# Half of the first batch's k and q before the rest, halved light attention, and new planner constants in a fused attention and feed-forward kernel

## The chip, the cores and the metric

The kernel runs on one core of a Trainium2 chip. The metric is the device time of one execution in microseconds (us); three timed runs are given by their median. A core has five engines that run side by side, each its own list of instructions in order: TensorE (PE in the profile, with its weight loads as PEld), VectorE (DVE), ScalarE (ACT), GpSimd (POOL) and SyncE (SP), which here issues the loads, the stores and the DMA transposes. They wait for one another by semaphores. PE writes to PSUM, which has eight banks in this kernel, all of them named; the other data lie in SBUF.

## The reference

Sliding window attention feeds a feed-forward block with a squared ReLU. There are 8 batches of 576 tokens, 8 heads of 64.

```python
scores = scale * np.matmul(q, k.transpose(0, 1, 3, 2))          # scale 1/8
mask = np.abs(pos[:, None] - pos[None, :]) <= 32
scores = np.where(mask, scores, -1000000000.0)
scores = scores - np.max(scores, axis=-1, keepdims=True)
attn = np.exp(scores)
attn = attn / (np.sum(attn, axis=-1, keepdims=True) + 1e-09)
x = np.matmul(attn, v)                  # then to (4608 tokens, 512)
h = x @ w_in                            # 512 x 2048
r = np.maximum(h, 0.0)
g = s * (r * r) + b
return (g @ w_out).astype(np.float32)   # 2048 x 512
```

All inputs and the output are float32. The kernel computes the matrix products in bfloat16. It uses that s and b are scalars: out = s * (r*r @ w_out) + b * (column sums of w_out).

## The kernel before

**Tiles.** The 4,608 tokens form 36 attention tiles of 128 (index j). The feed-forward part takes six tiles of 128 tokens and then fifteen of 256. The first product (`ht`, line 1015) is done in groups of 16 matmuls of 128 columns or 8 of 256; ACT takes the ReLU of a group (line 1024), DVE squares it into GT (line 1043). The second product (line 1063) is done in four groups of four matmuls per 128 tokens, one for each quarter of w_out; DVE scales it and adds the constant (line 1077), SP stores it. The column sums of w_out (line 940) need all of w_out.

**Weights.** w_in and w_out are loaded as float32 in four chunks of 1 MB each (i0 to i3, o0 to o3), into parts of GT or of the output buffers that are not in use yet, and are cast to bfloat16 by four casts a chunk. `WSET` (line 291) names the engines that may cast: ACT and POOL. The next chunk in the same place waits for the casts of the one before.

**The first batch.** k and q of batch 0 come as raw float32 (`load_raw`, line 568): partition h*16 + c holds 36 consecutive tokens of head h. Each of k and q is loaded in two halves, a half holding 18 tokens out of each 36. They are cast by eight pieces of 288 columns (`turn_raw`, line 577), turned by matmuls against a permutation matrix PERM in five groups, and copied into TURN (`kwt`, `qwt`), where the tokens lie along the free dimension. Every tile of the first batch that reads TURN waits for all of it (`turns`, line 673).

**Attention.** Tiles 0 to 2 use `attend_light` (line 681): scores with the mask added by a matmul, one maximum per row (DVE, line 704), the same scores transposed, from which the maxima are taken off by a small matmul (line 740), exp on ACT straight into the transposed form (line 746), row sums by matmuls, then the product with v, one division (line 775), a turn back (line 782) and a copy to XT. Even and odd heads lie in two PSUM banks, but each step takes both. The other tiles use `attend` (line 793): DVE adds the mask and takes the maximum for each head (line 832), ACT takes exp and the sum (line 840), POOL or, in the first five tiles, also DVE multiplies by the reciprocal (line 854), and P is transposed by PE for tiles below `PDMA` and by a DMA transpose on SP's queue from there on (line 868). k and q of later batches are cast by POOL (`cast_kq`), v by POOL or DVE (`cast_v`, line 636); for tiles below 12 a second copy VO of v with the halves exchanged is made by ACT or DVE (`make_vo`, line 641).

**What sets the order.** All work is entered as nodes with a cost in ns, a key, and what it reads and writes. `_Plan.order` (line 103) lays the nodes out engine by engine: whenever an engine is free by its own clock, it takes the ready node with the smallest key; a node with several engines (`move`, line 547) goes to the one that would finish it first. The result is a fixed list for each engine; on the chip each engine goes through it in order. `akey(j)` (line 305) is the key of attention tile j, min(640, 600 + 60j) tokens ahead of the same tokens' first product. `room` (line 112) models how many DMA descriptors SP may have outstanding, `RING`, `ISSUE` and `LAND` (line 25) how long a load takes. `FIRST` (line 289) is the order of the first loads: K0 is the first half of k, v0 the first tile of v; what stands behind the n-th bar is entered with tile n-1's attention. Where PE would idle early, filler matmuls (line 462) are put in.

## Time and profile before

| what | value |
|---|---|
| timed runs | 317.75 us median of 3 (317.01 to 319.76) |
| profiled execution | 316.46 us |
| its span, first to last instruction | 314.7 us |
| granted TensorE clock | 1.00 throughout |
| PE, DVE, ACT, POOL busy | 300.8, 229.0, 230.0, 145.5 us |
| moved by DMA | 61.82 MB |

The profiled execution's own time is 316.46 us: 1.8 us lie around its span. Busy times are sums over the span; matmuls overlap one another, so a busy PE may still be doing little. In the rows by stage, the columns are the stage, its length, and the busy time of each engine with the number of instructions in brackets, then the granted clock, the share of the 16 DMA engines' time (which can pass 1) and GB/s. In the rows in order of time, the first number is the start, the second how long the piece lasts; brackets at the end give how long the engine was idle before it and what it waited for. "x16" counts instructions merged into a row.

### The profile page before, as it was taken

The numbers are of one execution on the slowest core, as the hardware profiler recorded it, in microseconds if no ns is written. First come the engines' busy times: TensorE is split into PE (matmuls) and PEld (weight loads), VectorE is DVE, ScalarE is ACT, GpSimd is POOL, SyncE is SP. The second block draws the span as 40 slices with busy tenths as digits, with TensorE's granted clock in tenths as the row PEclk, the third lists the DMA queues.
The fourth block names the chain that finished last, engine by engine and source line by source line (L and its number), as shares of the span: only waits on it lengthen the run. The fifth ranks groups of instructions, "written<-read, shape, count | busy, mean of one in ns | idle before, by whom it ended". The sixth has DMA issues, their size and how long they took to land.

```text
span 314.7 us, 10141 instructions
## 1 busy us (share of the span) xinstructions
PE 300.8 (96%) x3936; PEld 207.4 (66%) x3981; DVE 229.0 (73%) x897; ACT 230.0 (73%) x747; POOL 145.5 (46%) x192
## 2 busy tenths in 40 slices
PE   7899899998999999999999999999999999999996
PEld 3468657586667665776666766666666666676674
DVE  5779499899998778677766787678858767653242
ACT  5577866899797868698787878798878778835230
POOL 7233476556575534445454654655654532220000
PEclk9999999999999999999999999999999999999999
DMA  7998999999999999999999999899999562220011
GB/s 273 359 351 228 361 268 214 240 229 179 210 213 210 232 187 197 223 227 176 191 218 226 210 205 233 217 192 226 225 247 204 123 149 70 70 67 35 33 69 68
DMA packets 157125, 61.82 MB, mean 196 GB/s; under 512 B 131220, under 2 KB 147988, under 8 KB 157076
## 3 DMA queue, kind: packets, MB, share of 16 engines
q1 hardware_dynamic: 157072, 61.16, 90.7%
q8 instruction: 31, 0.51, 0.7%
q14 instruction: 18, 0.15, 0.2%
q10 hardware_dynamic: 4, 0.00, 0.0%
HBM read 37.03 MB, written 9.44 MB: 148 GB/s over the span
## 4 chain that ended last, share of the span: by engine, by line
PE 77%; DMA 7%; DVE 7%; ACT 3%; POOL 2%; issue 2%; SPq 1%
PE ht L1015 35%; PE ptp L1063 15%; PE outp L1063 15%; DMA gt<-in_moe_w_out_dram 3%; PE sc L820 3%; DMA v<-in_v_dram 2%; ACT p L840 2%; PE sc L1063 2%; DMA r32k<-in_k_dram 2%; PE av L1063 2%; DVE ss L832 1%; PE tp L909 1%; PE av L915 1%; DVE mx L704 1%; DVE outs L1077 1%
## 5 line engine op out<-in xcount | busy, mean ns | idle before, releaser
L1015 PE MATMUL ht<-xt,win 128*128 128x256 bf16 (+1 forms) x1344 | 146.5, 257 | 0.0
L1015 PEld LDWEIGHTS ht<-xt,win 128*128 128x128 bf16 x1344 | 115.1, 98 | 32.7
L1024 ACT ACTIVATE r<-ht 128x512 bf16<-128x512 f32 x144 | 85.1, 592 | 47.3 <-PE ht L1015 45.8
L1043 DVE TENSOR_TENSOR gt<-r 128x512 bf16<-128x512 bf16 x144 | 83.6, 583 | 48.7 <-ACT r L1024 47.1
L840 ACT ACTIVATE p<-ss,mx 128x128 bf16<-128x128 f32 x264 | 110.0, 420 | 7.6 <-DVE mx L832 6.9
L854 POOL TENSOR_TENSOR p<-p,rc 128x512 bf16<-128x512 bf16 x64 | 70.0, 1114 | 77.5 <-DVE rc L849 77.5
L832 DVE CUSTOM_DVE_ANT_0 ss<-sc,mask 128x128 f32<-128x128 f32 x264 | 62.0, 280 | 8.8 <-PE sc L820 8.4
L1063 PE MATMUL outp<-wout,gt 128*128 128x512 bf16 (+1 forms) x246 | 63.0, 372 | 3.9 <-issue 1.7
L1063 PE MATMUL ptp<-wout,gt 128*128 128x512 bf16 x240 | 61.9, 379 | 1.7 <-issue 1.3
L840 ACT ACTIVATION_READ_ACCUMULATOR p<-ss,mx 128x1 f32 x264 | 50.2, 190 | 0.0
L1063 PEld LDWEIGHTS outp<-wout,gt 128*128 128x128 bf16 x272 | 24.9, 98 | 19.3 <-ACT wout L556 1.0
L1063 PEld LDWEIGHTS ptp<-wout,gt 128*128 128x128 bf16 x256 | 24.1, 98 | 19.3
L551 POOL CAST kn<-r32k 128x512 bf16<-128x512 f32 x34 | 21.1, 646 | 23.9 <-DMA r32k<-in_k_dram 23.9
L551 POOL CAST qn<-r32q 128x512 bf16<-128x512 f32 x32 | 21.3, 665 | 9.9 <-DMA r32q<-in_q_dram 9.5
L832 DVE DVE_READ_ACCUMULATOR2_ANT mx<- 128x1 f32 x264 | 20.8, 79 | 0.0
L924 ACT COPY half<-tp 128x512 f32<-128x512 f32 x24 | 14.0, 583 | 9.2 <-PE av L915 8.8
L551 POOL CAST ve<-v 128x512 bf16<-128x512 f32 x27 | 18.0, 667 | 3.3 <-PE av L915 2.5
L926 DVE TENSOR_TENSOR xt<-av,half 128x512 bf16<-128x512 f32 x24 | 16.3, 681 | 0.9 <-ACT half L924 0.8
L820 PEld LDWEIGHTS sc<-kt,qt 64*64 64x64 bf16 x768 | 10.8, 108 | 8.7 <-issue 7.8
L820 PE MATMUL sc<-kt,qt 64*64 64x64 bf16 (+1 forms) x768 | 14.2, 204 | 0.0
L846 DVE TENSOR_SCALAR sm<-sm 128x8 f32<-128x8 f32 x33 | 6.7, 202 | 8.9 <-ACT p L840 8.8
L1077 DVE SCALAR_TENSOR_TENSOR outs<-outp,scb,cvec 128x512 f32<-128x512 f32 (+1 forms) x17 | 12.4, 728 | 0.9 <-PE outp L1063 0.9
(142 smaller groups left out, 237.3 us busy)
## 6 DMA issues: line engine op xcount, KB each, us to landing
out_dram<-outs SPq DMA_DIRECT2D x35, 256.0 KB, 3.8
v<-in_v_dram SPq DMA_DIRECT2D x28, 256.0 KB, 5.5
r32q<-in_q_dram SPq DMA_DIRECT2D x28, 256.0 KB, 5.2
r32k<-in_k_dram SPq DMA_DIRECT2D x9, 512.0 KB, 4.7
gt<-in_moe_w_in_dram SPq DMA_DIRECT2D x4, 1024.0 KB, 10.6
gt<-in_moe_w_out_dram SPq DMA_DIRECT2D x3, 1024.0 KB, 9.7
v<-in_v_dram SPq DMA_DIRECT2D x8, 192.0 KB, 5.1
r32k<-in_k_dram SPq DMA_DIRECT2D x3, 448.0 KB, 4.8
```

Of the source, the lines that this page charges most:

```text
L551: return e.tensor_copy(dst, src)
L820: r = e.matmul(SC[hh][64 * u:64 * u + 64, pr, x0:x1], lhsT=qq, rhs=kk, start=True, stop=True)
L832: lambda e, ss=ss, x=x, y=y, pr=pr, hh=hh: e.tensor_tensor_reduce(out=SS[ss][:, x, :], in0=SC[hh][:, pr, :], in1=MASK[kind][:, :], scale=- ...
L840: lambda e, ss=ss, x=x, y=y: e.activation(P[pb][:, y, :].rearrange("q (a p t) -> q a p t", a=2, t=2), spread(SS[ss][:, x, :]), AF.Exp, bia ...
L854: return e.tensor_tensor(P[pb][:, y0:y0 + 4, :], P[pb][:, y0:y0 + 4, :], RC[mb][:, y0:y0 + 4].unsqueeze(2).broadcast_to([128, 4, 128]), AL ...
L924: add("act", lambda e: e.copy(HALF[hb][:, :], AV2[:, :]), 620, key + AVK, reads=[AV2N], writes=[("HALF", hb)])
L926: add("dve", lambda e: e.tensor_tensor(XT[:, :, 128 * (j % NX):128 * (j % NX) + 128], AV[:, :, :], HALF[hb][:, :].rearrange("p (a b) -> p ...
L1015: r = e.matmul(hbank[:, nt * f:nt * f + nt], lhsT=WIN[:, kc, 128 * ft:128 * ft + 128], rhs=XT[:, kc, x0:x0 + nt], start=(kc == 0), stop=(k ...
L1024: return e.activation(R1[rb][:, :], hbank[:, :], AF.Relu, bias=0.0, scale=1.0)
L1043: return e.tensor_tensor(d, r, r, ALU.mult)
L1063: r = e.matmul(op_[:, 0:cn], lhsT=GT[:, g_, fc, :], rhs=WOUT[:, fc, c0:c0 + cn], start=(fc == 0), stop=(fc == 15))
L1077: add("dve", lambda e, ob=ob, op_=op_, c0=c0, cn=cn: e.scalar_tensor_tensor(OUTS[ob][:, 0:cn], op_[:, 0:cn], SCB[:, 0:1], CVEC[:, c0:c0 + cn],
```

## The change

- **Loads of the first batch.** A half of k or q is now a half of the tokens: first 288 tokens, then the other 288. The 16 chunks of 18 tokens are the outer dimension, the heads the inner one, so a partition is c*8 + h and PERM is built for that. The order of the loads is Q0, K0, K1, v0, v1, Q1 instead of K0, K1, Q0, Q1, v0, v1. Each half is cast and turned by itself, in three groups of 6 tokens; tiles 0 and 1 wait only for the first halves, and the second halves get later keys. The bfloat16 copies lie where P and the scores lie later, not in XT.
- **Order of the loads after that.** v4 goes from before o0 to before o3; q4 and q5 come after k2 and before o1.
- **Light attention by halves.** Each step of `attend_light` is split into one for the even heads and one for the odd ones; the row sums move into the same bank as the product with v.
- **Who does what.** Weights may also be cast by DVE, the VO copies by POOL too; casts of v from tile 12 on are POOL's alone; POOL may take squares of the first four tiles; PE's transposes of P go up to tile 4 instead of 3 (`PDMA` 5); DVE's share of the normalisation goes up to tile 5.
- **The scalars s and b** are spread over the partitions after tile 1's attention instead of at the start.
- **Planner.** Costs of most operations are changed (ACT's ReLU 490 instead of 600, DVE's square 400 instead of 440, and so on), the latency behind an instruction is 230 instead of 130 (190 on POOL), a load lands after 1200 instead of 2000, a queue entry counts in full until it is done. There is a rule to leave an engine idle for a better node that is ready soon, switched off by `LOOK` = 0. The lead of attention is min(640, 500 + 40j).

What the built lists of the instructions show:

| engine | before | after |
|---|---|---|
| DVE: casts of weights | 0 | 16 |
| ACT: casts of weights | 16 | 7 |
| POOL: casts of weights | 16 | 9 |
| POOL: casts and copies of v | 27 | 40 |
| DVE: casts and copies of v | 25 | 14 |
| SP: DMA transposes of P | 32 | 31 |
| PE: filler matmuls | 16 | 10 |

```diff
-START, RING, ISSUE, LAND = 800.0, 2400.0, 700.0, 2000.0
+START, RING, ISSUE, LAND = 800.0, 2400.0, 700.0, 1200.0
-HOLD, DEFER, CHANGE = 800.0, 200.0, 97.0
+HOLD, DEFER, CHANGE = 100.0, 200.0, 97.0
+LOOK, LOOK_GAP, LOOK_END = 0.0, 50.0, 30000.0
...
-            while sum(q * min(1.0, (end - t) / dur) for end, dur, q in queue if end > t) + nd > RING:
+            while sum(q for end, dur, q in queue if end > t) + nd > RING:
...
-    LEAD, L0, LS = 640, 600, 60
-    RELU, SQ = 500, 200
-    FIRST = "K0 K1 Q0 Q1 v0 v1 i0 i1 i2 v2 i3 v3 v4|q4 o0 k2 o1 o2 q5 o3|v5|||"
+    LEAD, L0, LS = 640, 500, 40
+    NSQ = 4
+    RELU, SQ = 300, 400
+    FIRST = "Q0 K0 K1 v0 v1 Q1 i0 i1 i2 v2 i3 v3 o0 k2|q4 q5 o1 o2 v4 o3 v5||||"
-    WSET = {"i": ("pool", "act"), "o": ("act", "pool")}
-    NFLEX, TAIL = 8, 3
-    PDMA, KQDMA, AHEAD, GATE = 4, 11, 4, 5
-    CKEY, SKEY = 200, -9250
+    WSET = {"i": ("pool", "act", "dve"), "o": ("act", "pool", "dve")}
+    VOP = 12
+    HSTEP, CB, VOK = 0.1, -500, -100
+    NFLEX, TAIL = 10, 3
+    PDMA, KQDMA, AHEAD, GATE = 5, 11, 4, 5
+    CKEY, SKEY = 100, -9450
-    WHOLE, LIGHT, CH, NDIV = 4, 3, S // 16, 5
+    HC, HT_ = -600, 150
+    WHOLE, LIGHT, CH, NDIV = 4, 3, S // 16, 6
...
     def VSET(j):
-        return ("pool", "dve")
-    def OSET(j):
-        return ("act", "dve")
+        return ("pool",) if j >= 12 else ("pool", "dve")
+    def OSET(j, r0):
+        return ANY if r0 == 0 and j < VOP else ("act", "dve")
...
-            src = {"K": k, "Q": q}[x][0].rearrange("h (c r) d -> (h c) (r d)", r=CH)
+            src = {"K": k, "Q": q}[x][0][:, S // 2 * half:S // 2 * half + S // 2, :].rearrange(
+                "h (c r) d -> c h (r d)", c=16)
...
+        def turn_raw(x, half):
+            flat, out, late = FLAT[x], TURN[x], 0 if x == "K" else 50
+            step, n = CH * D // 8, CH // 6
+            ckey_, tkey = (-9500, -9400) if half == 0 else (HC, akey(2) - HT_)
...
-        turns = [("TURN", x, i) for x in "KQ" for i in range(5)] + ["KPAD"]
+        def turns(j):
+            return ["KPAD"] + [("TURN", x, half, i) for x in "KQ" for half in range(2 if j > 1 else 1)
+                               for i in range(3)]
...
+            for hh in range(2):
+                h_ = hh * HSTEP
+                pts = [("PTS", ptb, y) for y in range(hh, 8, 2)]
+                turned[j] = add("pe", partial(av, hh=hh), 500, key + 3 + h_,
...
+                add("dve", lambda e, hh=hh: e.reciprocal(RC[mb][:, hh:8:2], AVB[hh][:, 256:260]), 120,
...
-                    add("act", relu, 600, key - RELU, reads=[hres], writes=[("R1", rb)])
+                    add("act", relu, 490, key - RELU, reads=[hres], writes=[("R1", rb)])
...
-                add("dve", sq, 440, key - SQ, reads=[("R1", rb)],
+                few = t0 < 128 * NSQ
+                add(("dve", "pool") if few else "dve", {"dve": sq, "pool": sq} if few else sq,
+                    {"dve": 400.0, "pool": 1100.0} if few else 400, key - SQ, reads=[("R1", rb)],
```

## The prediction

> **What bounds the kernel now.** I read the page first (who is busy, and the chain that ended last), then the busy time by stage, then the chain and the instructions in order of time over the first 48 us.
>
> ```profile
> span 314.7 us, 10141 instructions
> ...
> PE 300.8 (96%) x3936; PEld 207.4 (66%) x3981; DVE 229.0 (73%) x897; ACT 230.0 (73%) x747; POOL 145.5 (46%) x192
> ...
> PE 77%; DMA 7%; DVE 7%; ACT 3%; POOL 2%; issue 2%; SPq 1%
> ```
>
> The stages (length, PE, PEld, DVE, ACT, POOL, granted clock, DMA share, GB/s) say where the missing share of PE is:
>
> ```profile
> 10.00:15.00 5.00, 4.21 (x98) 1.99 (x97) 3.96 (x10) 1.84 (x4) 0.26 (x1) 1.00 1.07 379
> 15.00:20.00 5.00, 4.25 (x94) 2.62 (x95) 3.05 (x8) 3.26 (x6) 2.34 (x4) 1.00 1.09 378
> ...
> 25.00:30.00 5.00, 5.00 (x104) 4.58 (x103) 4.96 (x21) 4.24 (x10) 2.22 (x4) 1.00 0.85 233
> ...
> 35.00:40.00 5.00, 4.07 (x51) 3.03 (x50) 1.93 (x5) 3.97 (x13) 1.99 (x3) 1.00 1.09 376
> ...
> 60.00:80.00 20.00, 18.59 (x312) 13.69 (x314) 19.05 (x86) 18.33 (x70) 14.03 (x18) 1.00 1.14 219
> ...
> 100.00:140.00 40.00, 39.31 (x490) 26.93 (x496) 30.48 (x139) 32.24 (x116) 20.17 (x25) 1.00 1.15 210
> ```
>
> From 100 us to 300 PE is idle for about 2% of the time: there only less PE work would help. PE's gaps lie at 35 to 40 us (0.93), at 60 to 80 us (1.41, with DVE at 95%), and before 21 us, where the "busy" PE mostly runs filler and short attention matmuls. The chain over the start tells what it waits for:
>
> ```profile
> 2.78 7.43 DMA v<-in_v_dram
> ...
> 11.65 0.60 PE sc L691 x2
> ...
> 21.39 1.89 PE ht L1015 x32
> ...
> 26.98 9.68 DMA gt<-in_moe_w_out_dram
> ...
> 36.69 1.14 ACT wout L556 x2
> ```
>
> The first work of the large products (the first product, ht) starts at 21.39; then the loads of w_out set the end until about 44 us. So the change can win in two places only: an earlier first product, and less lost around the w_out chunks. Whatever is won must survive 45 to 80 us, where DVE (37.4 of the 40 us from 40 to 80) has hardly any slack.
>
> **1. Halves of the tokens.** Before, tile 0's scores need all four raw loads. In order of time, POOL finds the second load at 6.24 and the third at 7.65; the first is there by 5.14, the fourth at 9.25, each a half of 0.59 MB. After, tiles 0 and 1 need Q's first half (first in the queue, by 5.1) and K's first half (second, 6.24).
>
> ```profile
> 6.24 1.05 POOL L551 CAST xt<-gt 128x288 bf16<-128x288 f32 x1 [0.68 <-DMA gt<-in_k_dram]
> ```
>
> Then: three casts on DVE at 0.24 apart (four take 0.95) to 6.95; turns of 12 matmuls (16 take 0.44); three copies of 384 columns, all on ACT's queue, at about 0.37 each (512 columns come 0.49 apart), to about 8.3. Scores at about 8.5 instead of 11.65: 3.2 us earlier. But not all of it arrives. In DVE's new order, tile 0's reciprocal and division stand behind two casts of w_in's first chunk, which DVE did not have before. That chunk keeps its place in bytes (4 raw halves and two v tiles ahead of it), so it lands as now:
>
> ```profile
> 15.17 1.14 ACT L556 CAST win<-gt 128x512 bf16<-128x512 f32 x2 [3.08 <-DMA gt<-in_moe_w_in_dram]
> ```
>
> From 15.17 DVE does, in its order: two casts (0.84), two reciprocals (0.2 each), two divisions of half size (0.35 each), a reduction (0.61), four small operations (0.17 each), two casts of the second chunk (17.66 is its landing now; 0.84), then the copy to XT (0.42): about 19.3. The first product starts at about 19.5: **1.9 us earlier**, 3.2 at most, 0 if DVE comes late. The chunks behind it (cast at 17.66, 20.22, 24.27) are not moved by the change, so the second and third groups of tile 0 wait for nothing new.
>
> **2. w_out and what PE does meanwhile.** The new load order puts w_out chunk 0 ahead of v4 and q4 (256 KB each): now cast at 31.5, then about 28.3. Chunk 1 has v3, k2, q4, q5 ahead of it instead of v3, v4, q4, k2: the same bytes. So its cast (36.69), chunk 2's (39.52) and 3's (43.38) move little. At 23 to 28 us DMA falls to 0.85 share (233 GB/s) with three loads of 256-byte rows in a row; the new order has k2, q4, q5 in a row instead. I take 0.4 us earlier, bounds 0 and 1.3.
>
> PE's order around these chunks: before, two groups each of chunk 0, then chunk 1 at 38.03, and up to chunk 3's first group at 47.05: with 12 groups of first product done by then. After: all of tile 3's turn, tile 4's q turn and scores and one more group of first product (0.93) stand ahead of chunk 1, where PE has the 1.9 us to do them; behind it stand chunk 1 (two groups, 1.73), chunk 2 (1.73, not before 39.5 and its casts), tile 3's second product of attention (0.5), two groups of ht (1.75), then the column sums, which need chunk 3: its casts end about 44.2, the sums take 0.97: chunk 3's first group at 45.2 instead of 47.05. Together 1.85 + 0.93 = 2.8.
>
> The casts themselves: 4 per chunk, now two on ACT beside two on POOL (1.14 and 1.17). After: mostly two on DVE (0.42 each), one each on ACT and POOL (0.61). Beside each other that would be 0.84, one after the other on DVE and POOL 1.45. The row above (POOL's cast beside DVE's: 1.05 instead of the 0.42 of the cast at 5.14) and the next one lie nearer to one after the other:
>
> ```profile
> 39.74 2.01 DVE L1043 TENSOR_TENSOR gt<-r 128x512 bf16<-128x512 bf16 x2
> ```
>
> (two squares of 0.42 beside POOL's 1.54 for P). I take 1.45, that is 0.3 later: 2.8 - 0.3 + 0.4 = **2.9 us**. The Trainium skill (SBUF — State Buffer, "Who interferes with whom") says the same against this change: DVE and GpSimd share one port pair, and an exclusive lock makes the later of the two wait for the whole instruction; these rows agree. By that rule 0.3 is lost per chunk; if they ran freely the sum would be 3.5.
>
> **3. Tile 4's P by PE (PDMA 5).** Eight transposes more on PE (0.45) and a copy on DVE (0.68 at 41.67); one DMA transpose less on SP, whose queue holds the loads (1.29 of issue at 67.19). The chain after that issue is a load of k of 6.41, POOL's casts, and PE's longest gap of this stretch, 1.04 at 77.58 waiting for POOL's qn. I set the 0.45 off against half that gap: 0, bounds -1.0 and +0.45.
>
> **4. Who does what.** In all, DVE loses five casts of v, six copies of v for VO, two copies of kt, three of kwt/qwt, and gains 16 casts of weights, two half normalisations of P and the halves' small operations; ACT loses nine casts of weights; POOL loses seven and gains 13 of v. DVE's gain in work is before 45 us, where it stands idle (1.93 of 5 busy at 35 to 40; 2.6 us in one wait); its loss is behind, where it is full. I cost it at 0; if the gaps of 45 to 80 us all went it would be -1.7, without that cover +3 (rival 3).
>
> **5. Constants of the planner.** They act through the order only. From tile 5 on, the first and second product stand within half a tile of the old place at each tile's scores (before tile 20's: 16.75 and 14.75 tiles in both), and the last 27 groups of PE are the same. 0, bounds -1.5 and +1.5 (PE's gaps from 80 to 300 us are some 3.7 in all).
>
> **Sum.** 314.7 - 2.9 = 311.8 of span; 1.8 lie around it in the profiled run (316.46): 313.6. That run is 1.3 under the median of the timed ones (317.75), which would give 314.9. I forecast between the two: **314.3 us**.
>
> **Rivals.**
> 1. *Hidden by the w_out loads* (316.0 to 317.5, say 317). PE arrives earlier at chunk 1 and only waits longer. For it: chain and a DMA share of 1.09 at 35 to 40. Against it: one more group and three small pieces of PE work stand ahead of the wait. Then 0.93 - 0.45 is all that remains.
> 2. *More goes than the start* (about 311). The 1.3 of DMA, the 1.7 of 45 to 80 us and 1.0 later go too: 2.9 + 3.2 to 4. For it: DVE is relieved just where it is at 95%. Against: POOL gets 13 casts and DVE's squares wait beside POOL.
> 3. *DVE stuck behind weights* (about 321, slower). DVE never waited for a weight; now it meets eight chunks in order, with squares, maxima and XT behind them. From 40 us on DVE has 2.6 us of slack, and the 2.9 won must go first as well: it decides where these waits sum to over 5.5 us more than in the walk above. At 1 us for each chunk of w_in and 1.25 for each of w_out they are 9, so 3.5 slower. Against: by the rows, DVE comes to the chunks within 1 us of their landing.
> 4. *The halves don't land earlier.* If the raw loads with the new row order took twice their 1.5 us, all weights would be 6 us later: about 322. For it nothing in the trace; the rows stay 4,608 bytes long, and 16 chunks are outermost.
>
> **Chances.** Forecast 0.50 (own range 312.4 to 316.2), rival 1 0.20, rival 2 0.13, rival 3 0.14, rival 4 0.03. A measurement here tells about 1% from no change; 1% under 317.75 is 314.6. Two thirds of the forecast and rival 2 lie below: faster 0.46; the rest of the forecast and rival 1: same 0.37; rivals 3 and 4: slower 0.17. Range 310.8 to 318.0: rivals 3 and 4 are outside.
>
> **What would show it.** Scores of tile 0 at 8 to 9.5 and first ht at 19 to 20 (step 1); w_out chunk 0 cast by 29, chunk 3 still near 43, its first group at 44.5 to 46 (step 2); no DVE wait for a weight over 2 us; windows from 100 us as now. Wrong if ht starts at 21 or later, if DVE waits long for weights, or if the gaps between 45 and 80 us grow.

## The result, and the profile after

| | before | after |
|---|---|---|
| median of 4 runs each, us | 318.29 (317.01 to 319.76) | 329.06 (327.97 to 332.36) |
| profiled execution: time, span | 316.46, 314.7 | 328.9, 327.2 |
| mean granted clock in it | 1.00 | 0.974 |

The ratio is 1.0379, with a 95% interval of 1.0332 to 1.0427: by it the change costs 12 us (10.8 between the medians), where I had forecast a gain of 3.4. Where executions of one kernel differ in their granted clock, ratios in this document are of those less disturbed by that, and the others' times are given beside them.

The page of the changed kernel, in the lines that answer those shown of before, and the row of the granted clock in 40 slices of 8.2 us:

```profile
span 327.2 us, 10182 instructions
...
PE 310.3 (95%) x3943; PEld 214.1 (65%) x3989; DVE 231.1 (71%) x915; ACT 227.6 (70%) x746; POOL 146.9 (45%) x193
...
PEclk9856999999999999999999999999999999999999
...
PE 75%; DVE 14%; ACT 4%; DMA 3%; issue 2%; POOL 1%; SPq 0%; DVEq 0%
```

PE is busy for 9.5 us more with the same work, which suggests that it ran slower somewhere, and the clock row says where. Before, that row held 9 throughout. DVE's share of the chain went from 7% to 14%. The stages (columns as before):

```profile
10.00:15.00 5.00, 3.42 (x72) 2.17 (x67) 3.53 (x10) 2.56 (x6) 1.73 (x3) 0.84 1.17 228
15.00:20.00 5.00, 4.99 (x72) 3.17 (x71) 1.65 (x7) 2.48 (x5) 0.48 (x1) 0.50 1.04 396
...
25.00:30.00 5.00, 5.00 (x57) 3.43 (x52) 2.46 (x6) 1.37 (x3) 2.55 (x5) 0.50 0.47 143
...
35.00:40.00 5.00, 5.00 (x109) 4.51 (x106) 4.55 (x27) 4.90 (x16) 2.36 (x4) 1.00 1.26 238
...
60.00:80.00 20.00, 19.62 (x295) 13.86 (x297) 16.05 (x70) 15.13 (x57) 9.94 (x14) 1.00 0.77 183
100.00:140.00 40.00, 38.75 (x438) 26.60 (x443) 30.78 (x127) 30.70 (x107) 21.08 (x27) 1.00 1.14 212
```

And from 5 to 10 us, first before, then after the change:

```profile
5.00:10.00 5.00, 3.94 (x120) 2.56 (x121) 4.31 (x15) 3.80 (x9) 3.33 (x7) 1.00 1.09 366
5.00:10.00 5.00, 3.36 (x76) 2.20 (x75) 1.73 (x5) 2.24 (x7) 1.13 (x2) 1.00 1.03 231
```

Three things are new. At 5 to 10 us, with the raw halves on their way, the DMA engines are as busy as before (1.03, before 1.09) but move 231 GB/s instead of 366. (At 10 to 15 us it is 228 instead of 379, but there the changed kernel still loads raw rows and v's 256-byte rows, and the kernel before already w_in, so these two don't compare the same load.) From 15 to 30 us the clock stands at 0.50. At 25 to 30 us the DMA engines are half idle (0.47). The chain of waits over the start:

```profile
2.16 8.74 DMA gt<-in_k_dram
...
12.30 0.32 PE sc L701
...
28.70 1.82 PE ht L1048 x16
...
55.18 2.00 DVE wout L554 x2
```

The first product starts at 28.70 instead of 21.39, and between 11.73 and 28.70 this chain has no gap: PE itself is the bound. Chunk 3 of w_out has its first group at 58.45 instead of 47.05, so 11.4 of the 12.5 us of span are lost by then.

### The profile page after: what moved, and what is told of

Read it like the earlier page. It is cut to its first block, busy times and chain, and to the rows that moved or that the text cites. A ratio compares the mean times of both kernels' runs of the same rounds, so it can differ in the third digit from the quotient of the medians.

```text
span 327.2 us, 10182 instructions
## 1 busy us (share of the span) xinstructions
PE 310.3 (95%) x3943; PEld 214.1 (65%) x3989; DVE 231.1 (71%) x915; ACT 227.6 (70%) x746; POOL 146.9 (45%) x193
## 4 chain that ended last, share of the span: by engine, by line
PE 75%; DVE 14%; ACT 4%; DMA 3%; issue 2%; POOL 1%; SPq 0%; DVEq 0%
PE ht L1048 31%; PE outp L1098 14%; PE ptp L1098 14%; DVE gt L1076 3%; ACT p L852 3%; PE sc L832 3%; DMA gt<-in_k_dram 3%; DVE ss L844 2%; PE sc L1098 2%; PE av L1098 2%; DVE wout L554 1%; ACT r L1057 1%; DVE vo L554 1%; DVE xt L912 1%; PE tp L921 1%
## 5 line engine op out<-in xcount | busy, mean ns | idle before, releaser
L1048 PE MATMUL ht<-xt,win 128*128 128x256 bf16 (+1 forms) x1344 | 148.9, 259 | 1.6 <-DVE xt L912 0.8
L1076 DVE TENSOR_TENSOR gt<-r 128x512 bf16<-128x512 bf16 x144 | 81.3, 566 | 41.5 <-ACT r L1057 40.0
L844 DVE CUSTOM_DVE_ANT_0 ss<-sc,mask 128x128 f32<-128x128 f32 x264 | 62.5, 280 | 10.4 <-PE sc L832 10.2
L554 POOL CAST ve<-v 128x512 bf16<-128x512 f32 x32 | 21.8, 683 | 12.3 <-PE av L927 6.1
L1112 DVE SCALAR_TENSOR_TENSOR outs<-ptp,scb,cvec 128x512 f32<-128x512 f32 x16 | 11.9, 741 | 3.0 <-PE ptp L1098 3.0
```

The costliest lines, as they stand in the source:

```text
L554: return e.tensor_copy(dst, src)
L844: lambda e, ss=ss, x=x, y=y, pr=pr, hh=hh: e.tensor_tensor_reduce(out=SS[ss][:, x, :], in0=SC[hh][:, pr, :], in1=MASK[kind][:, :], scale=- ...
L1048: r = e.matmul(hbank[:, nt * f:nt * f + nt], lhsT=WIN[:, kc, 128 * ft:128 * ft + 128], rhs=XT[:, kc, x0:x0 + nt], start=(kc == 0), stop=(k ...
L1076: return e.tensor_tensor(d, r, r, ALU.mult)
L1112: add("dve", lambda e, ob=ob, op_=op_, c0=c0, cn=cn: e.scalar_tensor_tensor(OUTS[ob][:, 0:cn], op_[:, 0:cn], SCB[:, 0:1], CVEC[:, c0:c0 + cn],
```

## The experiments

I set up these theories. **A**: the raw loads' row order, 16 chunks outermost, halves their rate, and all follows. **B**: my third rival, DVE behind the weights. **C**: the clock at half rate carries the loss. **D**: PE's queue has the wrong order, made from load times that are too short. **E**: a late PE holds back weight casts, so slots, so w_out's loads. "Clock held" means granted at 1.00 from 12 to 60 us, but for 3.4 us at most.

### The loads' row order

The kernel with the rows of before:

```diff
-            src = {"K": k, "Q": q}[x][0][:, S // 2 * half:S // 2 * half + S // 2, :].rearrange(
-                "h (c r) d -> c h (r d)", c=16)
+            src = {"K": k, "Q": q}[x][0].rearrange(
+                "h (c r) d -> (h c) (r d)", r=CH)[:, lo:hi]
```

> The changed kernel with one thing undone: the four loads of the first batch's k and q read the rows in the order of the kernel before (head and chunk as one dimension of 128 rows, stepping 9,216 bytes, the halves being halves of each row's tokens). Every instruction, its place on its queue and its cost stay those of the changed kernel; what is left out is that the partitions then hold other tokens, so k and q of the first batch come out with their tokens in another order. Theory A (the row order with 16 chunks outermost halves the rate of these loads, 322 ns against 178 ns a packet, and everything else follows from that: PE idle, its clock down to 0.50 from 14 to 30 us, the casts of w_out late): packets of 4,608 bytes back at about 180 ns, K's first half landed by 6.5 us instead of 8.38, Q's second by 11.5 instead of 15.74, granted clock 1.00 from 14 to 30 us, the first ht at 19.5 to 21.5 instead of 28.70, chunk 3's first group at 45 to 48 instead of 58.45, time 314 to 318. Theory B (my third rival: with w_in and w_out cast on DVE too, DVE stands behind the weights whenever they come): the landings are early as in A, but the column sums still wait for DVE, chunk 3's first group comes after 52, time 321 to 325. Theory C (only the clock: PE fell under what keeps it at full rate because of the order of the turns, not the loads): the landings are early, but the clock still falls to 0.50 for over 5 us, time 322 to 328.

Measured: the median of the 512 packets of 4,608 bytes is 178 ns again, as before, where the changed kernel has 322. K's halves land at 7.27 and 9.14 instead of 8.38 and 10.92, Q's second at 12.47 instead of 15.74. But the clock falls all the same, for 30.7 us, and the time is 329.26 (325.6 to 331.3; ratio 1.0281, 1.0147 to 1.0416). So A is right on the loads and wrong that all follows from them.

The other way round, the kernel before with the chunks outermost (the same rearrangement, `r=CH`, and PERM's pattern changed):

> The kernel before with one thing done: its loads of the first batch's k and q put the 16 chunks outermost (partition = chunk, head; the halves remain halves of each chunk's 36 tokens; the permutation of the turn is changed to match). Same instructions, same order. Theory A: its packets of 4,608 bytes take about 320 ns instead of 178, the four loads land 2 to 5 us later (Q's second half at 15 to 16), the weights behind them too, PE idles and its clock falls to 0.50 for some us, and the time rises to 322 to 330 from 318. Theory B: the loads may land later, but with the order of the kernel before DVE has no weight casts in the way: 318 to 321. Theory C (the clock falls because of the new order of the turns): clock 1.00 throughout, 318 to 322.

Measured: 327 ns a packet, the four loads found at 5.67, 8.19, 10.71 and 13.26 by the casts, the clock at 0.50 for 10.2 us, and 320.93 us: ratio 1.0095 (1.0055 to 1.0134). The row order costs some 3 us in the kernel before, clock included.

### The clock

Fillers where PE waits, by a first guess:

```diff
-                def fn(e, at=at, bank=bank):
+                def fn(e, at=at, bank=bank, more={("Q", 0, 0): 3, ("K", 0, 0): 5, ("K", 1, 1): 7}.get(
+                        (x, half, i), 0)):
+                    fill(e, "attn", more)
...
```

Beside these, products of zeros add to the scores' banks: 8 and 5 in `scores_t`, 8 in `scores`.

> The changed kernel with more fillers on PE in the first 15 us: 3 matmuls of 512 columns ahead of the first turn of Q, 5 ahead of K's, 7 ahead of the second turn of K's second half, 8 and 5 zero products behind the transposed scores of tiles 0 and 1 and 8 ahead of the second scores of tile 1. The loads keep the row order with 16 chunks outermost. Theory A (the slow loads are the cause, the clock one of their results): the clock stays at 1.00 at 14 to 30 us, the loads land where they did (K's first half at 8.4, Q's second at 15.7), and the time comes down by the PE work that ran at half rate, as far as it stood on the path: first ht at 22 to 25 instead of 28.70, chunk 3's first group at 50 to 55 instead of 58.45, time 319 to 325. Theory C (the clock alone carries the loss): time 315 to 318, as before. Theory B (DVE behind the weights): first ht early, but chunk 3's first group stays at 56 to 59 and the time at 326 to 329.

The clock held, and the time was 328.17 (1.0321, 1.0244 to 1.0398). This looks like the end of C, but the chain of waits of this kernel shows what I had built:

```profile
11.80 1.69 PE ht L488 x7
...
16.73 1.83 PE outp L477 x8
...
22.17 1.73 PE sc L477 x8
...
26.72 1.19 PE outp L477 x5
...
30.09 1.00 PE ht L1061 x16
```

The fillers stand on the path, 6.4 us of them. From the first of them to the first ht are 18.3 us, all PE's but for 0.7; without the fillers it would be 11.9, against 17.0 in the changed kernel. So the half rate costs up to 5 us by this point, and even at full rate the first ht would be at 23.6, behind the 21.39 of before. Next, nine fillers only where PE stood idle:

```diff
+MORE = {"mm": 0, "fm": 3, ("Q", 0, 2): 1, ("K", 0, 2): 5}       # after these pieces of PE's queue
```

> The changed kernel with nine more fillers, all put behind a piece of PE's queue after which PE stands idle anyway: 3 behind the last transposed mask (idle from 5.25 to 6.37 us), 1 behind Q's first turn, 5 behind the turn of K's first half (idle from 10.15 to 11.73). Order, loads and all else unchanged. From the runs before: with the fillers that were tried first, the chain from K's second half landing (10.98) to the first ht (30.09) had no gap and held 6.4 us of those fillers themselves; without them it would be 11.9 us of PE work, against 17.0 in the changed kernel with the clock at 0.50. Theory C (the clock at half rate carries most of the loss): clock 1.00 from 12 us, first ht at 23 to 24.5 instead of 28.70, chunk 3's first group at 51 to 54 instead of 58.45, time 320 to 324. Theory D (beside the clock, the order on PE's queue: the turns of K's second half ahead of tile 0's scores, all turns and most of tile 2's scores ahead of the first ht): the time stays at least 2 us over that of the kernel before (318), as the first ht still comes 2 us later than its 21.39. Theory B (DVE's casts): chunk 3's first group stays after 56 and the time above 326. If it falls to 318 or under, the clock was all.

They held the clock only until 19.7; then it fell for 13.7 us (330.02, ratio 1.0368, 1.0297 to 1.0439). That settles nothing on C. What the clock costs is answered by a pair without the halves, which I come to, and by this one: the kernel before without the fillers that its planner puts into PE's waits (`FILL = ()`).

> The kernel before without the fillers that its planner puts into PE's waits (the seven ahead of all work stay). It prices the clock by itself: same loads at full rate, same casts, same order but for the 9 fillers. Theory C (PE keeps its clock only while it is busy enough in the first 12 us, and at half rate its work up to the first w_out chunks stretches): granted clock 0.50 for 5 us or more between 8 and 30 us, time 321 to 329. If the clock stays at 1.00, or falls and the time stays at 317 to 319, the clock is not what costs the changed kernel its 11 us.

The clock falls, for 10.2 us in the profiled execution, and the median is 319.23 (1.0028, 0.9994 to 1.0063): nothing that can be told. Its four executions with the lowest mean clocks, 0.967 to 0.973 (by that some 17 to 21 us at half rate, an estimate), took 318.4 to 321.2, and the three at 0.999 to 1.00 took 318.9 to 319.5. In the kernel before, the clock is cheap.

### All but the halves

The changed kernel with the rows and the order of the first loads of before, so that tile 0 needs all four:

```diff
-    FIRST = "Q0 K0 K1 v0 v1 Q1 i0 i1 i2 v2 i3 v3 o0 k2|q4 q5 o1 o2 v4 o3 v5||||"
+    FIRST = "K0 K1 Q0 Q1 v0 v1 i0 i1 i2 v2 i3 v3 o0 k2|q4 q5 o1 o2 v4 o3 v5||||"
-            ckey_, tkey = (-9500, -9400) if half == 0 else (HC, akey(2) - HT_)
+            ckey_, tkey = -9500, -9400
...
```

> The changed kernel without the halves of tokens: the first batch's k and q are loaded as in the kernel before (rows of head and chunk, K's halves then Q's, all four needed by tile 0), with all else of the changed kernel: its planner, its costs and due times, w_in and w_out cast on three engines, chunk 0 of w_out called for early. Theory A: the landings of the kernel before (K's first half at about 6.2, Q's second at 10 to 11), the clock at 1.00, first ht at 20 to 22, chunk 3's first group at 45 to 48, time 314 to 318. Theory B: landings as in A, yet tile 0 stands behind the w_in casts on DVE and chunk 3's first group comes after 51: 321 to 325. Theory C (the order of the turns): clock 1.00 as all four are needed at once, as in the kernel before: 315 to 319.

Ten executions fall into two groups: three with a mean clock of 0.995 to 1.00 take 317.7 to 319.3 (ratio 1.0021, 0.9964 to 1.0078), seven with 0.953 to 0.973 take 323.5 to 329.1. So the rest of the change costs little while the clock holds, and a fallen clock in it up to 11 us. To make that an experiment, the same kernel with more fillers and with none:

```diff
-FILL, FILL_MIN, FILL_SHARE, FILL_NS = ("attn", "sums"), 400.0, 0.5, 220.0
+FILL, FILL_MIN, FILL_SHARE, FILL_NS = ("attn", "sums"), 150.0, 0.9, 220.0      # more
+FILL, FILL_MIN, FILL_SHARE, FILL_NS = (), 400.0, 0.5, 220.0                    # none
```

> The changed kernel without the halves (rows and order of the loads of the kernel before, all four needed by tile 0), with more fillers: 0.9 of each planned wait instead of 0.5, from 150 ns up (some 19 instead of 8 up to the first ht). Theory C: clock 1.00 in every execution, time 316.5 to 319.5, where the same kernel with fewer fillers lay between 317.7 and 329.1. That would leave the planner, the casts on three engines and the rest of the change at no gain and no loss. If DVE's casts or the planner's constants cost anything at full clock, it stays over 320; if they gain, under 316.

> The changed kernel without the halves and without the planner's fillers (the seven ahead of all work stay). Its clock should fall to 0.50 for 8 us or more in the first 35 us, as in the kernel before without fillers, where that cost 0.8 us at the median. Theory E (the clock is dear in the changed kernel because its casts of w_in's last two chunks stand on ACT and DVE behind the attention of one more tile: a slow PE then holds back the slots, the issue of w_out's loads and so chunk 3): 325 to 330, with the first load of w_out issued at 25 us or later instead of 21.9 and chunk 3's first group after 50. Rival: the clock costs the same here as there, 318 to 321.

With more: 319.75 (1.0063, 1.0029 to 1.0098), all ten between 317.5 and 321.0. With none: 327.47 (1.0326, 1.026 to 1.0392). Without fillers the changed order of work loses 7.7 us, and that of before 0.8; but in the changed order the fall is also three times as long. The first two rows are the kernel without halves and fillers, the other two the kernel before without fillers:

```profile
30.00:35.00 5.00, 5.00 (x71) 3.89 (x68) 3.17 (x9) 1.83 (x3) 0.62 (x1) 0.50 1.16 271
35.00:40.00 5.00, 5.00 (x55) 4.41 (x50) 1.62 (x9) 0.60 (x1) 2.29 (x4) 0.50 0.89 284
```

```profile
20.00:25.00 5.00, 5.00 (x62) 3.59 (x57) 3.01 (x7) 2.19 (x4) 2.21 (x4) 0.50 1.06 274
25.00:30.00 5.00, 5.00 (x92) 4.31 (x90) 2.75 (x9) 3.08 (x6) 1.49 (x3) 0.76 0.95 287
```

In the kernel before the clock is back at 27 to 28 us; in the changed order it stays down till 40 us (30.7 us in all). What is seen beside it: before puts 32 matmuls of ht in a row (3.60 us at half rate, at 23.23), shortly ahead of the clock's return; the changed order puts 16 (1.89) between pieces of attention, at 26.14, 31.13 and 36.22, and the clock is back only after 16 and 16 at 36.22 and 38.33. Whether this is why was not tried.

### The order on PE's queue

In the changed kernel PE's queue, in order of time, reads:

```profile
9.69 0.46 PE L600 MATMUL ptp<-perm,ss 128*64 128x64 bf16 x12
11.73 0.57 PE L600 MATMUL ht<-perm,ss 128*64 128x64 bf16 x24 [1.58 <-DVE ss L554]
12.23 0.39 PE L701 MATMUL sc<-maskb,ident 128*128 128x512 bf16 x1
...
18.37 0.61 PE L701 MATMUL sc<-maskb,ident 128*128 128x512 bf16 x1
```

The 24 matmuls turn K's second half. Tile 0's scores (L701) need none of it, but stand behind it in the list and wait 1.58 us for its casts. (The same mask matmul takes 0.39 at 12.23 and 0.61 at 18.37: full and half rate.) The planner counts 1,450 ns for a raw load; they follow one another at 2.5 to 2.7 us. Told 2,500, it puts the scores first and 8 fillers instead of 2 ahead of them:

```diff
-    RAWNS = 1450
+    RAWNS = 2500
```

> The changed kernel with one constant of its planner changed: it counts 2,500 ns for each of the first batch's raw loads instead of 1,450. In the changed kernel's profile these loads follow one another at 2.2 to 2.8 us. By the order that comes out, tile 0's scores then stand ahead of the turns of K's second half on PE's queue, and the planner puts 8 fillers ahead of them instead of 2. Loads and their rows unchanged. Theory D (the order, made from load times that are too short, is the cause, and with it the missing fillers): clock 1.00 from 12 us on, tile 0's scores at about 10.5 instead of 12.23, first ht at 21 to 23, chunk 3's first group at 47 to 50, time 316 to 320. Theory C: the clock is kept, time 320 to 324, no better than fillers alone. Theory A (the slow loads themselves): clock kept, but all weights still come 4.3 us late: chunk 3's first group not before 51, time 320 to 322. Theory B: above 324.

The four executions: 321.9 with the clock at 1.00, and 326.5, 329.3 and 329.8 with 0.97 to 0.98 (the ratio, 1.0184 with an interval of 1.0059 to 1.0308, mixes the two). In the first, which was profiled, scores came at 10.34 and first ht at 21.92, as D expected; chunk 3 at 50.73 and the time lie beyond D's ranges, next to A's (51, and 320 to 322). Between executions of this one kernel a fallen clock goes with 4.6 to 7.9 us, and with it the mended order is hardly faster than the changed kernel (328.0 to 332.4). With the fillers raised to 0.9 as well:

> The changed kernel with its planner told 2,500 ns for a raw load (as before), and in addition allowed to fill 0.9 of each planned wait of PE instead of 0.5, from 150 ns up instead of 400: 18 fillers stand before tile 0's scores' end instead of 9 (2, 4, 8 and 4 behind the first seven). Same order, same loads. Where the same order ran at a clock of 1.00 from 12 to 60 us it took 321.9 us; where it fell to a mean of 0.97 or 0.98 it took 326.5 to 329.8. Theory C (the clock is what makes these executions differ): clock 1.00 in every execution, 320 to 323.5 throughout, so 5 to 7 us faster than the median of 327.9. If the clock stays at 1.00 and the time is still 326 or more, the clock was a companion and not the cause. Theory A: not under 320, since the raw loads still land at 5.9, 8.4, 11.0 and 15.8 us and w_in's chunks 4 us late.

Three executions with the clock held: 322.7, 323.2 and 324.7 (1.0192, 1.0118 to 1.0266); one at 0.979, which is the profiled one: 328.4. So with order and clock mended, some 6 us remain. The slow loads are in it.

### Casts and slots

The kernel with nine fillers, w_in and w_out cast by POOL and ACT alone:

```diff
-    WSET = {"i": ("pool", "act", "dve"), "o": ("act", "pool", "dve")}
+    WSET = {"i": ("pool", "act"), "o": ("act", "pool")}
```

> The kernel with nine fillers in PE's idle time, and in it one more part of the change undone: the casts of w_in and w_out go to POOL and ACT alone, as in the kernel before, and DVE has none of them. Theory B (DVE behind the weights): at least 3 us faster than the same kernel with the casts on three engines, no wait of PE for DVE at the column sums, 316 to 320. Theories C and D: within 1.5 us of the kernel with the casts on three engines, either way (ACT and POOL take 0.61 a cast, four of them two by two 1.2 us instead of 0.85 to 1.45).

331.75 (1.0389, 1.0297 to 1.0482), against 330.02 with three engines. The clock was down for 27.3 us here and for 13.7 there, so it is no clean test, but nothing in it speaks for B. Without DVE, ACT's half of w_in's third chunk came at 29.85 (POOL's at 24.44), and w_out's first load was issued at 31.00: the cast stands behind attention on ACT too. The same edit on the kernel without halves, clock held:

> The changed kernel without the halves, with 0.9 of each planned wait of PE filled (which took 1.0063 of the kernel before, clock at 1.00), and with w_in and w_out cast by POOL and ACT alone, as in the kernel before. Theory B (DVE's casts of the weights cost what is lost): ratio 0.996 to 1.002, the first load of w_out issued before 23 us. Otherwise (the casts find room on DVE and would only stand behind attention on ACT instead): 1.003 to 1.012, that load at 24 us or later.

1.0112 (1.006 to 1.0164) against 1.0063 with three engines: taking DVE off the weights gains nothing, and B falls. For E, w_out's chunk 0 in a buffer that is free from the start:

```diff
-    SLOT = dict(i0=0, i1=1, i2=2, i3=3, o0=2, o1=3, o2=4, o3=2)
+    SLOT = dict(i0=0, i1=1, i2=2, i3=3, o0=4, o1=2, o2=3, o3=4)
```

> The changed kernel with w_out's chunks in other slots: chunk 0 in the output staging buffer (slot 4), which is free from the start, chunks 1 and 2 in slots 2 and 3, chunk 3 in slot 4 again. Loads, casts, fillers and the rest of the order unchanged. Theory E (the slots: a late PE holds back the casts of w_in's third chunk and so the issue of w_out's first load): that load is issued at 21.5 to 24 us instead of 29.99, the DMA engines no longer stand idle from 27 to 31.5, w_out's later chunks are issued 3 to 6 us earlier each, chunk 3's first group comes at 52 to 55.5 instead of 58.45, time 322.5 to 326. If only PE's own longer work counts: the load is issued earlier, but chunk 3's first group stays after 57 and the time at 327.5 to 330.

The first load was issued at 22.07 instead of 29.99 and the DMA engines had no gap (1.10 at 25 to 30 us), but chunk 3's first group came at 61.90 and the time was 330.15 (1.0338, 1.0294 to 1.0383). The clock was down for 34.1 us there, 17.1 in the changed kernel, so it is no clean test of E. It shows that the place is what the load waits for, and that an early first load alone doesn't bring chunk 3 forward.

### The halves, mended

Heads outermost and chunks inside, a load time of 2,000 and fillers at 0.9:

```diff
-                "h (c r) d -> c h (r d)", c=16)
+                "h (c r) d -> h c (r d)", c=16)
-    RAWNS = 1450
+    RAWNS = 2000
...
```

> The changed kernel with its three faults mended: the token halves are loaded with the 8 heads outermost and 16 chunks inside (partition = head, chunk; the permutation changed to match), so that 16 rows in a row lie 4,608 bytes apart (73,728 in all) instead of 147,456 apart; the planner is told 2,000 ns for a raw load; and it fills 0.9 of each wait. Theory A (only the row order with chunks outermost is slow): packets at about 180 ns, K's first half at 7.3, its second at 9.1, Q's second at 12.5 as with the rows of the kernel before; scores of tile 0 at about 9.5, first ht at 18.5 to 20.5, w_in and w_out where they were in the kernel before, clock 1.00: 313.5 to 317. That is what I had forecast of the change. If the halves do not pay even so: 317 to 320. If the heads outermost are as slow as the chunks: 320 to 323.

336.54 (1.0615, 1.0539 to 1.0691): far worse. Of this kernel:

```profile
5.00:10.00 5.00, 1.49 (x36) 0.99 (x37) 0.75 (x3) 0.89 (x3) 0.00 (x0) 0.80 0.82 156
10.00:15.00 5.00, 3.70 (x54) 1.84 (x51) 1.30 (x4) 1.57 (x5) 0.00 (x0) 0.50 0.51 135
```

The DMA engines are 0.51 busy where they should be full, and the halves land at 8.65, 13.38, 17.60 and 25.64. The Trainium skill (DMA: Bandwidth & Descriptors, "Why a DMA increments its semaphore by 16 and not by 1", on how many engines) says that a DMA runs on the largest number of engines up to 16 that divides the slowest dimension on both of its sides. By that, 8 heads outermost get 8 engines and 16 chunks 16, and the share here agrees. Nor are the packets fast again, as I had expected: their median is 304 ns. So both orders tried for a half of the tokens are slow, one with the DMA engines half idle, the other at 322 ns a packet; a third was not tried. What the halves would bring with fast loads can still be seen with rows of before, order and clock mended:

> The changed kernel with its raw loads reading the rows in the order of the kernel before (so that the partitions hold other tokens: k and q of the first batch come out with their tokens in another order, which is left so), its planner told 2,000 ns for a raw load, and 0.9 of each planned wait of PE filled. So the halves come at full rate, tile 0's scores stand ahead of the turns of K's second half, and PE is kept busy. If my forecast of the halves was right as far as they are concerned: Q's first half landed at 4.6, K's first at 7.3 and second at 9.1, scores of tile 0 at 9 to 10, first ht at 18.5 to 20.5, chunk 3's first group at 44 to 46.5, time 313.5 to 317. If the halves do not pay even so, because PE then has all four turns and most of tile 2's scores ahead of the first ht: first ht at 20.5 to 22, chunk 3's first group at 46.5 to 49, time 317 to 320. If the clock falls in spite of the fillers: 323 or more.

322.78 (1.0086, 1.0043 to 1.0129; the kernel before took 319.7 beside it). Scores at 10.00, first ht at 20.80, only 0.6 us ahead of before. And then, of this kernel, the casts of w_in's third chunk and the first load of w_out:

```profile
20.91 0.61 POOL L554 CAST win<-gt 128x512 bf16<-128x512 f32 x1 [2.85 <-DMA gt<-in_moe_w_in_dram]
25.21 1.16 DVE L554 CAST win<-gt 128x512 bf16<-128x512 f32 x2
26.40 0.37 SPq L505 DMA_DIRECT2D gt<-in_moe_w_out_dram  x1
```

POOL has the chunk at 20.91, DVE 4.3 us later, and the load that needs its place waits: before it was issued at 25.25. Chunk 3's first group is at 51.13. With the casts on POOL and ACT:

> The kernel with fast halves and held clock (rows of the kernel before, so that the partitions hold other tokens and the first batch's k and q come out with their tokens in another order; 2,000 ns for a raw load; 0.9 of each planned wait filled; 1.0086 of the kernel before), and with w_in and w_out cast by POOL and ACT alone. Theory B: w_in's third chunk is cast within 1.5 us of its landing at about 20.9, w_out's first load issued at 22.5 to 24 instead of 26.40, chunk 3's first group at 47 to 49 instead of 51.13, ratio 0.993 to 1.001: then DVE's casts are what took the halves' gain. Otherwise, since on ACT too the casts of the third and fourth chunk stand behind exponentials and relus of tiles that come later: that load at 25.5 us or later, ratio 1.005 to 1.014.

First ht at 19.39, which is my forecast's 19.5, and w_out's first load at 23.71. Yet the ratio is 1.0104 (1.0032 to 1.0176; one execution of six, at a clock of 0.978, took 326.1). The gain dies on the way:

```profile
23.81 1.36 POOL L554 CAST win<-gt 128x512 bf16<-128x512 f32 x2 [1.82 <-DMA gt<-in_moe_w_in_dram]
...
27.76 1.13 ACT L559 CAST win<-gt 128x512 bf16<-128x512 f32 x2
```

and, by stage:

```profile
25.00:30.00 5.00, 3.27 (x79) 2.99 (x67) 4.96 (x26) 4.04 (x14) 1.32 (x3) 1.00 0.98 299
30.00:35.00 5.00, 4.21 (x86) 3.89 (x82) 4.81 (x13) 3.83 (x14) 3.45 (x6) 1.00 0.93 177
```

ACT casts w_in's fourth chunk 4 us after POOL (it stands behind two ReLUs, tile 2's exp and the first two of tile 3; before it stood behind tile 1's exp and two ReLUs and came at 24.27, with the landing), so w_out's second load goes out at 29.52 instead of 26.98. And DVE is full from 25 to 35 us, while PE waits 2.5 of the 10. Chunk 3's first group is at 50.30, 3.3 later than before.

### Tile 4's P

Without halves, more fillers, and `PDMA` 4 as before:

> The changed kernel without the halves, with 0.9 of each planned wait filled (1.0063 of the kernel before), and with the P of tile 4 turned by a DMA transpose again (PDMA 4) instead of eight transposes on PE and a copy on DVE. My step 3 put this part at 0, bounds -1.0 to +0.45 us: the ratio then stays within 1.003 to 1.0095. If the eight transposes and the copy stand on the path, 0.7 us faster or more: under 1.003.

318.13 (0.9991, 0.9958 to 1.0025), against 1.0063 (1.0029 to 1.0098) with `PDMA` 5: some 2.3 us, from two intervals that nearly meet. The list as a whole moves with it, so which instruction costs this is open.

### All together

Half rate: us at a clock of 0.50 in the first 60 us of the profiled execution. Other columns: us from the start.

| kernel | ratio | half rate | scores | first ht | w_out's first load issued | chunk 3's first group |
|---|---|---|---|---|---|---|
| before | 1 | 0 | 11.65 | 21.39 | 25.25 | 47.05 |
| before, no fillers | 1.0028 | 10.2 | 11.91 | 23.23 | 24.27 | 48.96 |
| before, chunks outermost | 1.0095 | 10.2 | 15.76 | 25.94 | 29.53 | 51.53 |
| no halves, fillers unchanged | 1.0021 | 0 | 11.82 | 20.82 | 21.90 | 46.64 |
| no halves, clock held, PDMA 4 | 0.9991 | 0 | 13.25 | 23.14 | 23.72 | 48.74 |
| no halves, clock held | 1.0063 | 3.4 | 13.24 | 23.73 | 24.31 | 49.33 |
| no halves, no fillers | 1.0326 | 30.7 | 13.41 | 26.14 | 26.77 | 58.40 |
| fast halves, clock held | 1.0086 | 3.4 | 10.00 | 20.80 | 26.40 | 51.13 |
| the same, two cast engines | 1.0104 | 0 | 8.81 | 19.39 | 23.71 | 50.30 |
| true load time | see above | 0 | 10.34 | 21.92 | 27.06 | 50.73 |
| after | 1.0379 | 17.1 | 12.23 | 28.70 | 29.99 | 58.45 |

With 318 us for the kernel before, the 12 us come apart like this. All but the halves: 2.0 (1.0063), no more than what went with PDMA 5. Halves at full rate, clock held: 0.7 more (1.0086). Slow loads on top: 3.4 (1.0192), in line with the 3.0 in the kernel before. The rest, 6.0, is what an order made for 1,450 ns a load and the half rate that comes with it cost together; they were not parted in the changed kernel's own order. These are differences of ratios, and by their intervals the 0.7 can't be told from nothing, the 3.4 may be 0.7 to 6.1 and the 6.0 may be 3.1 to 8.7 (estimates).

Of the first 2.0, part may be the price of the added fillers. With the changed kernel's own fillers and the clock held, the kernel without the halves has chunk 3's first group at 46.64, ahead of before, and yet a span of 316.0 instead of 314.7: what it loses lies behind 47 us. No version here beats the kernel before.

## Why the prediction was wrong

**Step 1, the halves.** Four things failed. First, I took the landing of a second load (6.24) from the kernel before; with chunks outermost it was 8.38. This was my fourth rival, given 0.03 with "for it nothing in the trace". The trace of before could not show it, since no load in it has these rows; that is a reason for a wide bound, not for a small chance. The rival was priced at 6 us of lateness; the weights came 4.3 late, and it costs some 3.4.

Second, "scores at about 8.5": I walked along what tile 0 needs, not along PE's list. That list has the turns of K's second half ahead of the scores, and it could be read beforehand. Even with fast loads and the order mended, scores came at 10.00; at 8.81 only once DVE cast no weights either.

Third, I had DVE's casts of w_in hold tile 0 until 19.3 (my own terms add up to 19.7). That was not the limit. PE was, with 17.0 us of gapless work between K's second half and the first ht, since the list puts all turns and most of tile 2's scores there too. 1.9 us earlier was right only in the kernel with everything mended and no weight casts on DVE (19.39).

Fourth, I held that the change does not move w_in's other chunks. It does not in bytes. It does in the queues: a chunk's casts stand behind one more tile of attention on DVE and ACT.

**The clock** is in no step at all. The table ahead of the prediction has fillers going from 16 to 10, and I did not ask what they are for. The profile of before has a row of 1.00 throughout, and I took it for a property of the chip instead of something that the kernel keeps up. Together with the order that goes with it, it is the largest term of the loss, 6.0 of the 12 us; the two were parted only between executions of the kernel told 2,500 ns (321.9 with the clock held, 326.5 to 329.8 without).

**Step 2, w_out.** Forecast: chunk 0 cast at 28.3, chunk 3's first group at 45.2. Measured: 35.80 and 58.45; in the best mended case 29.60 and 50.30. What failed is that I counted the bytes ahead of each load: the loads are paced by the slots, that is by the casts of the chunk before in the same place, and these by attention. The 0.3 for DVE and POOL shutting each other out and the 0.4 of DMA can't be seen beside this. The 0.85 and 233 GB/s that I read for 23 to 28 us are those of 25 to 30 us; from 23 to 28 it is 0.77 and 140.

**Step 3, PDMA 5.** Taken at 0, bounds -1.0 and +0.45: measured, without the halves, about +2.3, outside.

**Step 4, who does what.** Taken at 0: about right, as far as the 0.9991 without halves and PDMA 5 shows it, which has steps 4 and 5 together. Rival 3, slower by DVE behind weights, had the sign and a price of 3.5 us, but not the mechanism: taking DVE off the weights gained nothing in any of three kernels (1.0389 for 1.0368, 1.0112 for 1.0063, 1.0104 for 1.0086).

**Step 5, the planner's constants.** "They act through the order only" holds, and from 100 us on the windows are as before (38.75 of 40 against 39.31). But the bounds of 1.5 us were made for the steady part. At the start the changed order came with a clock that, without fillers, stayed down for 30.7 us instead of 10.2.

**The rivals.** Rival 1, that w_out's loads hide what is won, is what was left of the halves when all else was mended: 2 us earlier at the first ht, nothing at chunk 3. For rival 2, that more goes than the start, no run has anything: the lowest ratio is 0.9991.

## What to carry to other kernels

Follow a moved step along the static list of each engine, not along its data: what stands ahead of it in the queue is its dependency too. A load with a new access pattern has a new rate; bound it widely until a trace shows it, and tell the planner what was measured. Keep TensorE's fillers through every change of the start, and read a fallen granted clock before anything else: here a fall of 10.2 us came with a loss of 0.8 us in one order of the work, and one of 30.7 us with 7.7 in another.

## What the runs showed of the hardware

- **Row order of a load.** The same 128 rows of 4,608 bytes take 178 ns a packet (median) with head and chunk as one dimension of 128 rows, 9,216 bytes apart; 322 or 327 with 16 chunks outermost and 8 heads, 147,456 bytes apart, inside them; and 304 with 8 heads outermost and 16 chunks, 4,608 bytes apart, inside them. The busy share of the DMA engines doesn't tell the first two apart (1.09 and 1.03 at 5 to 10 us), GB/s does (366 and 231). Why is not shown.
- **The clock goes in steps of 3.413 us.** The trace's record of the granted clock has stretches of 3.41, 10.24, 13.65, 17.07, 27.31, 30.72 and 34.13 us in these kernels: multiples of one length. The Trainium skill (TensorE: Matmul & The Clock Gate, "Part 1: The HAM clock gate") gives a free-running window of 3,413 ns in which activity is judged; the record agrees with the length. It also says that one busy window brings the full rate back. That does not fit these rows if busy is read from the profile: in the changed kernel PE is "busy" for 4.99 to 5.00 of each 5 us from 15 to 30 us and stays at 0.50 for 17.07 us, five such lengths. So busy time in the profile, here of attention's small matmuls, did not lift the clock; what does was not tried.
- **A row of 1.00 ahead of the first recorded change is no measurement.** The page shows 1.00 from the start on, while the first fillers come 0.43 us apart and later ones 0.22. In the kernel before the record starts at 6.14 us, so its "1.00 throughout" holds from there on. Two executions recorded at a mean of 1.00 were also as slow as their neighbours at 0.96 (327.3 and 329.8 us), so the mean alone doesn't tell a held clock.
- **Fillers cost time of their own.** Behind the wait they stand on the path (6.4 us in the first try). Ahead of it they are not free either: with 0.9 instead of 0.5 of the planned waits filled, the first ht of the kernel without halves stands at 23.73 instead of 20.82. There the clock was down for 3.4 us too, but with `PDMA` 4, the same fillers and the clock at 1.00 it is 23.14.
